# Attention, soft experts and a squared-ReLU layer on one core: another opening of the last stage, and sums moved to GpSimd

## The chip, the core and the metric

The kernel runs on one core of a Trainium2 chip. The metric is the device time of one execution in microseconds, the median of several runs; lower is better. TensorE multiplies matrices into PSUM, VectorE (DVE), ScalarE (ACT) and GpSimd (POOL) work elementwise, and SyncE (SP) issues the transfers. Each engine takes its instructions in the order in which they were put on its queue; semaphores tie the queues together.

## What is computed

Attention over 8 batches of 8 heads (576 positions of 64), causal in blocks of 64; then a soft mixture of 8 experts with 4 slots each over the 4608 tokens of width 512 (c is a softmax over the 32 slots); then a layer 512 to 2048 to 512 with a squared relu.

```python
def _attn_ref(q, k, v):
    ...
def _moe_ref(x, phi, w1, w2):
    ...
    for e in range(E):
        h = np.maximum(slot_input[e] @ w1[e], 0.0)
        slot_out[e] = h @ w2[e]
    ...
    return (c @ slot_out).astype(np.float32)
def _moe2_ref(x, w_in, w_out):
    h = np.maximum(x @ w_in, 0.0)
    return (h * h @ w_out).astype(np.float32)
def reference(**kwargs):
    ...
    attn_out = _attn_ref(**attn_kwargs)
    B, H, S, D = attn_out.shape
    x = np.ascontiguousarray(attn_out.transpose(0, 2, 1, 3)).reshape(B * S, H * D)
    x = _moe_ref(x=x, **moe_kwargs)
    return _moe2_ref(x=x, **moe2_kwargs)
```

## The kernel before

Three stages follow one another: attention (to about 430 us of the trace), the experts (to 464 us) and the last layer. Since the experts' output is a mixture of 32 slot outputs, the last layer's first product is done on the slots: `fold` (L1211) multiplies the slots' outputs with w_in into `psw`, a 128 x 512 tile in PSUM, from the copies `so` of the transposed sums (`finish`, L1203 and L1204). What is left per token is a product with the mixing weights.

**The last stage** (`ffn`). Of the 36 tiles of 128 tokens the first four (N0 = 4, 512 tokens) go through plain f32: `psw` is split into two rounded halves `wf0` and `wf1` (L1402, L1403, L1408, L1409), `spread` (L1418, L1421) brings them into the layout `ws`; for each chunk c = 0 to 7 of the hidden width `first_hidden` (L1441) makes 2 x 128 hidden rows, `relu_square` (L1430, L1431) makes g of them on ScalarE, and `first_product(c, a)` adds four products with the decoded w_out `t` into the four accumulators `pos` (`po`, L1626). Meanwhile w_out arrives and is decoded chunk by chunk (`decode_wo`, `decode_mag`: one ScalarE and four VectorE operations, L234 to L242, and a sum of magnitudes on ScalarE, jk, L1397).

The other 32 tiles form 16 blocks of 256 tokens, whose product with w_out is done in f16 high and low parts by a scheme of seven products in place of eight. It needs seven weight matrices of 128 x 2048: three are quarters of w_out itself, four are sums of quarters. `sum_w` makes the sums, one two-input subtraction of 2048 columns each: T3 writes the tile ta, T4 writes tb, T5 overwrites ta and T6 overwrites tb. `cast_w` (B, L1547, ScalarE) makes the high part bh of each with the scale beta, `low_w` (L, L1550, VectorE) the low part bl. For each block there are four quarters kq of the hidden width: `block_first` (H, L1568, tile ps_hb), `block_square` (q, ScalarE), `block_sums` (s: four sums of 256 columns), `block_cast` (c: ah, two ScalarE casts, the first of four parts, the second of three), `block_low` (l: al, two VectorE subtractions), and then the seven products (P, L1604) and their outputs (E; one sum per block on GpSimd, L1697). The tile pool of ps_h and ps_hb holds two tiles, so that a TensorE step for a third waits until ScalarE has read the first.

**What sets the order.** Under `manual_schedule` the string `ORDER` gives the order on TensorE, VectorE and ScalarE for the end of the first tiles and for the first block: a letter is a step, the digits its arguments (T3 is sum_w(3), q02 is block_square(0, 2), m40 is first_product(4, 0), h7 and g7 are first_hidden and first_square of chunk 7). GpSimd's order is left to the scheduler. The opening of the stage (from psw to chunk c=3) is written out in the code ahead of it, the first tile's work at the pace of ScalarE and VectorE copies:

```python
sub = lambda o, a, b: nc.vector.tensor_tensor(out=o, in0=a, in1=b, op=ALU.subtract)
...
x = tw[s] = tw["p"].tile([128, KH, HM], F32, tag=nm, name=nm) if s < 5 else tw[s - 2]
sub(x, a, b)
```

Of the kernel before, what the change touches and what calls it, by code (L numbers as in the profile page):

```python
# [23 lines left out]
def tile_attn_soft_moe_ffn(  # L24
# [12 lines left out]
    nc = tc.nc  # L37
# [23 lines left out]
    )  # L61
    NTILE = NT // 128
# [166 lines left out]
    def decode_mag(pool, dst, raw, w):  # L229
        hi, lo = raw[:, :, 1], raw[:, :, 0]  # L230
        m = pool.tile([128, w], F32, tag="dec_mag", name="dec_mag")
        b = m.bitcast(U32)
        with tc.high_priority():
            nc.scalar.activation(out=m, in_=hi.bitcast(F32), func=AF.Abs)  # L234
        nc.vector.tensor_scalar(out=m, in0=m, scalar1=2.0 ** -15, scalar2=None, op0=ALU.max)
        nc.vector.tensor_scalar(
            out=b, in0=b, scalar1=3, scalar2=0x3FFFFFF8, op0=ALU.logical_shift_left, op1=ALU.bitwise_and
        )
        nc.vector.scalar_tensor_tensor(
            out=b, in0=hi, scalar=0xC0000000, in1=b, op0=ALU.bitwise_and, op1=ALU.bitwise_or  # L240
        )
# [909 lines left out]
    def experts():  # L1151
# [144 lines left out]
    wos = {}  # L1296
# [67 lines left out]
    def ffn():  # L1364
# [19 lines left out]
        sc = {nm: ws_p.tile([128, 1], F32, name=nm) for nm in ("beta", "alpha", "inv", "sg", "se")}  # L1384
        sc.update(zip(("top", "sw"), cts["tiny"][2:]))
        al = [sc["alpha"]] + cts["tiny"][:2]
        wf = [d_p.tile([128, 512], F32R, name=f"wf{i}", bufs=1) for i in range(2)]
        tt = t_p.tile([128, KH, 2, DM], F32, name="t")

        def decode_wo(c, a=None):  # L1390
            sl = slice(0, 2) if a is None else slice(a, a + 1)
            w = DM * (sl.stop - sl.start)
            raw = wos[c][:, sl].rearrange("p a f x -> p (a f) x")
            decode_mag(d_p, tt[:, c, sl].rearrange("p a f -> p (a f)"), raw, w)
            if a != 0:
                jk = d_p.tile([128, 2, DM], mybir.dt.bfloat16, tag="jk", name="jk", bufs=1)
                nc.scalar.activation(out=jk, in_=tt[:, c], func=AF.Abs, accum_out=sums[:, c:c + 1])  # L1397

        psw = wots["psw"]
        parts = (slice(0, 128), slice(128, 512))  # L1400
        p = parts[0]
        nc.scalar.copy(wf[0][:, p], psw[:, p])  # L1402
        nc.vector.tensor_tensor(out=wf[1][:, p], in0=psw[:, p], in1=wf[0][:, p], op=ALU.subtract)  # L1403
        p = parts[1]
        wfs = cts["w"][:, p]
        nc.scalar.copy(wfs, psw[:, p])
        nc.scalar.copy(cts["w"][:, parts[0]], psw[:, parts[0]])
        nc.gpsimd.tensor_copy(wf[0][:, p], wfs)  # L1408
        nc.gpsimd.tensor_tensor(out=wf[1][:, p], in0=wfs, in1=wf[0][:, p], op=ALU.subtract)  # L1409
        decode_wo(0, 0)  # L1410
# [4 lines left out]
        def spread(c, p=slice(0, 512)):  # L1415
            ps = bank2("ps_ws")
            for i in range(2):
                nc.tensor.matmul(  # L1418
                    ps[:, p], cts["sel"][:, c, 32 * i:32 * i + 128], wf[i][:, p], start=(i == 0), stop=(i == 1)
                )  # L1420
            nc.scalar.copy(ws[:, 512 * c + p.start:512 * c + p.stop], ps[:, p])  # L1421
# [11 lines left out]
        def first_hidden(c, step=1024, late=False):  # L1433
            ps = bank2("ps_h")
            if late:
                hid[c] = lambda: first_square(c, ps)
            else:
                g = g_p.tile([128, 1024], F32, tag="g", name="g")
            for a in range(2):
                f = c + KH * a  # L1440
                nc.tensor.matmul(  # L1441
                    ps[:, 512 * a:512 * a + T0], ws[:, 128 * f:128 * f + 128], ctt[:, 0:T0], start=True, stop=True
                )
                if step == 512:
                    relu_square(ps, g[:, 512 * a:512 * a + 512], 512 * a, 512 * a + 512, scale=1.0 / CSC)
                    if a == 0:
                        spread(2, parts[0])
            if late:
                return
            if step == 1024:  # L1450
                relu_square(ps, g, 0, 1024, scale=1.0 / CSC)
            return g
# [83 lines left out]
        sub = lambda o, a, b: nc.vector.tensor_tensor(out=o, in0=a, in1=b, op=ALU.subtract)  # L1536
# [62 lines left out]
        def product(n, sa, sb, acc, first):  # L1599
# [10 lines left out]
        spread(0, parts[0])  # L1610
        hid = {0: first_hidden(0, 512)}
        decode_wo(0, 1)
        spread(0, parts[1])
        spread(2, parts[1])
        nc.vector.tensor_reduce(
            out=mg[:, 0:1], in_=wf[0].bitcast(F32), axis=AX.X, op=ALU.max, apply_absolute_value=True
        )
        spread(1)
        spread(3)
        for c in range(1, KH):  # L1620
            decode_wo(c)

        def first_product(c, a):
            g = hid[c]
            for t in range(N0):
# [166 lines left out]
```

## Time and profile before

| what | value |
|---|---|
| median of three runs | 865.24 us (864.58 to 865.53) |
| the profiled execution | 864.24 us, of which the span of the trace is 862.4 us |
| granted clock, mean | 0.991 of full speed |
| TensorE busy | 810.9 us, 94% of the span |
| VectorE, ScalarE busy | 670.2 us (78%), 626.9 us (73%) |
| GpSimd busy | 241.5 us (28%), nearly all in the attention stage |
| last stage | 464.2 us to the end |

A busy share says little by itself: the stages have different limits. A timeline row gives the start, the duration, the engine and line, the tiles, and in brackets the idle time before it with what ended it; rows that follow one another without a gap are merged and counted (x16). The chain lists, in order of time, what the last instruction of the kernel waited for, step by step. The granted clock of TensorE has two levels, 1.2 and 2.4 GHz; a slice in which it changed shows a value between 0.50 and 1.00.

### The profile page before, as it was taken

Reading aid. Unit: us, or ns where it says so; the run is one execution under the profiler, and the core shown is the slowest. Engines: PE = TensorE matmul, PEld = TensorE weight load, DVE = VectorE, ACT = ScalarE, POOL = GpSimd, SP = SyncE. Lnnn points to the kernel's source line nnn. Section 1 sums busy time; section 2 is a strip of 40 time slices with the busy share of each in tenths; the row PEclk is TensorE's granted clock in tenths of the full one; section 3 lists DMA queues with packets and bytes.
Section 4 is the critical chain, followed back from the end, with each engine's and each line's share of the span. In section 5 each row is a group of like instructions: output and inputs, shape, how many; then the busy total and the mean of one; then the engine's idle time right before and its main releaser. Section 6 shows DMA issues by size and latency. Waiting matters only on the chain.

```text
span 862.4 us, 21655 instructions
## 1 busy us (share of the span) xinstructions
PE 810.9 (94%) x8741; PEld 597.5 (69%) x8741; DVE 670.2 (78%) x1546; ACT 626.9 (73%) x996; POOL 241.5 (28%) x394
## 2 busy tenths in 40 slices
PE   2699999998999999999986999999999999999997
PEld 1366767575766667676432454888888888888886
DVE  5877789899899987764726899888888888888880
ACT  5588787787878687743225899988888888878770
POOL 0255747376574757464000000000000000000000
PEclk9899999999999999999998999999999999999999
DMA  7997998989898979589899100110000000000002
GB/s 156 194 192 132 186 216 151 223 160 224 156 215 163 197 124 197 90 251 373 335 401 397 57 0 25 39 37 25 26 25 27 25 26 25 26 25 26 26 25 49
DMA packets 213316, 113.14 MB, mean 131 GB/s; under 512 B 192096, under 2 KB 194144, under 8 KB 213216
## 3 DMA queue, kind: packets, MB, share of 16 engines
q1 hardware_dynamic: 210560, 111.11, 54.0%
q8 instruction: 68, 1.11, 0.5%
q10 hardware_dynamic: 2656, 0.66, 0.4%
q14 instruction: 32, 0.26, 0.1%
HBM read 78.71 MB, written 9.44 MB: 102 GB/s over the span
## 4 chain that ended last, share of the span: by engine, by line
PE 73%; DMA 8%; ACT 6%; POOL 6%; DVE 5%; issue 2%; SPq 0%; ACTq 0%; POOLq 0%
PE ps_y L1604 15%; PE ps_z L1604 10%; PE ps_x L1604 10%; PE xm L655 8%; PE ps_sc L581 6%; DMA t<-qb 4%; PE ps_hb L1568 3%; DMA wch<-in_moe_w_dram 3%; PE sm L675 3%; POOL ul L771 3%; PE ps_max L503 2%; POOL ss L624 2%; PE po L1626 2%; PE tl L666 2%; PE ps_qT L482 2%
## 5 line engine op out<-in xcount | busy, mean ns | idle before, releaser
L1604 PEld LDWEIGHTS <-ah 128*128 128x128 f16 x1792 | 174.8, 98 | 21.9 <-issue 0.8
L619 ACT ACTIVATE p<-ps_sc,es 128x512 f32<-128x512 f32 x192 | 129.7, 685 | 59.1 <-PE ps_sc L581 29.8
L1536 DVE TENSOR_TENSOR al<-a,ah 128x1024 f16<-128x1024 f32 (+1 forms) x128 | 138.5, 1124 | 16.9 <-ACT ah L1591 15.3
L517 DVE TENSOR_REDUCE pm<-ps_max 128x4 f32<-128x512 f32 x160 | 106.0, 681 | 32.6 <-PE ps_max L511 32.3
L624 POOL TENSOR_TENSOR ss<-p 128x384 f32<-128x384 f32 (+1 forms) x128 | 85.7, 688 | 152.4 <-ACT p L619 152.0
L1591 ACT CAST ah<-a 128x1024 f16<-128x1024 f32 (+1 forms) x128 | 114.4, 936 | 15.0 <-DVE a L1536 13.4
L581 PE MATMUL ps_sc<-t,s 128*128 128x512 f16 (+3 forms) x512 | 107.0, 302 | 11.7 <-DMA t<-qb 6.6
L1697 POOL TENSOR_TENSOR ot<-u,p 128x256 f32<-128x256 f32 x16 | 12.5, 781 | 373.6 <-DVE u L1668 357.9
L1604 PE MATMUL ps_y<-bh,al 128*128 128x256 f16 x384 | 104.7, 273 | 0.0
L1604 PE MATMUL ps_y<-bh,ah 128*128 128x256 f16 x384 | 104.6, 272 | 0.0
L1604 PE MATMUL ps_y<-bl,ah 128*128 128x256 f16 x384 | 104.6, 272 | 0.0
L624 POOL TENSOR_TENSOR ss<-ss,p 128x320 f32<-128x320 f32 (+1 forms) x128 | 97.9, 765 | 16.9 <-ACT p L619 9.1
L1604 PEld LDWEIGHTS <-al 128*128 128x128 f16 x896 | 87.6, 98 | 10.2
L1430 ACT ACTIVATE r<-ps_hb,cts_h 128x1024 f32<-128x1024 f32 x64 | 71.2, 1112 | 30.0 <-PE ps_hb L1568 29.4
L655 PE MATMUL xm<-p,ar_hi 128*64 128x256 f32 (+3 forms) x512 | 87.2, 440 | 0.0
L1536 DVE TENSOR_TENSOR a<-a 128x256 f32<-128x256 f32 x192 | 76.1, 424 | 3.9
L1604 PE MATMUL ps_x<-bh,ah 128*128 128x256 f16 x256 | 69.8, 273 | 0.0
L1604 PE MATMUL ps_z<-bh,ah 128*128 128x256 f16 x256 | 69.8, 273 | 0.0
L1604 PE MATMUL ps_x<-bh,al 128*128 128x256 f16 x256 | 69.8, 273 | 0.0
L1604 PE MATMUL ps_x<-bl,ah 128*128 128x256 f16 x256 | 69.8, 273 | 0.0
L1604 PE MATMUL ps_z<-bl,ah 128*128 128x256 f16 x256 | 69.8, 273 | 0.0
L1604 PE MATMUL ps_z<-bh,al 128*128 128x256 f16 x256 | 69.8, 273 | 0.0
(275 smaller groups left out, 1779.3 us busy)
## 6 DMA issues: line engine op xcount, KB each, us to landing
wch<-in_moe_w_dram SPq DMA_DIRECT2D x18, 1024.0 KB, 10.9
ar_hi<-in_v_dram SPq DMA_DIRECT2D x64, 128.0 KB, 3.8
raw<-in_moe_w_in_dram SPq DMA_DIRECT2D x16, 512.0 KB, 5.5
out_dram<-ot SPq DMA_DIRECT2D x32, 256.0 KB, 2.1
ar_hi<-in_moe_w_dram SPq DMA_DIRECT2D x6, 1024.0 KB, 7.8
s<-s SPq DMA_DIRECT2D x32, 144.0 KB, 4.1
ar_hi<-in_k_dram SPq DMA_DIRECT2D x16, 256.0 KB, 4.5
ar_hi<-in_q_dram SPq DMA_DIRECT2D x16, 256.0 KB, 4.2
```

The lines of the kernel that those rows point to most:

```text
L517: nc.vector.tensor_reduce(out=o, in_=i, axis=AX.X, op=ALU.max)
L581: nc.tensor.matmul(ps[:, c0:c0 + w].rearrange("p (s c) -> p s c", c=128), kk[:, 2 * t + hp, :], qq[:, 2 * u0 + hp:8:2, :], start=(c0 == 0 ...
L619: exps[:] = [nc.scalar.activation(out=pt, in_=ps, func=AF.Exp, scale=es[:, 0:1])]
L624: add = lambda o, x, y: nc.gpsimd.tensor_tensor(out=o, in0=x, in1=y, op=ALU.add)
L655: nc.tensor.matmul(box["xm"][64 * hp:64 * hp + 64, 128 * t:512], vs[:, t, hp, :], r, start=(t == 0), stop=(t == 3),)
L675: nc.tensor.matmul(SM[b][32 * g:32 * g + 32, o0:o0 + w], oj, r, start=bool(start and j == 0), stop=stop, tile_position=(0, 32 * g), skip_g ...
L771: add = lambda o, x, y: nc.gpsimd.tensor_tensor(out=o, in0=x, in1=y, op=ALU.add)
L1430: nc.scalar.activation(out=r[:, c0:c1], in_=ps[:, c0:c1], func=AF.Relu, **kw)
L1536: sub = lambda o, a, b: nc.vector.tensor_tensor(out=o, in0=a, in1=b, op=ALU.subtract)
L1568: nc.tensor.matmul(ps[:, 512 * j + 256 * a:512 * j + 256 * a + 256], w[:, 128 * f:128 * f + 128], c, start=True, stop=True,)
L1591: nc.scalar.copy(v(hl[n % 2][0][:, 2 * kq:2 * kq + 2], s), v(a7[n, kq], s))
L1604: nc.tensor.matmul(acc[:, 0:HM], a[:, k], b[:, k], start=bool(first and k + j == 0), stop=(k == KH - 1 and j == 2), skip_group_check=not f ...
```

## The change

It has four parts. (1) At the end of the experts the two pairs of transpositions and the folds are ordered anew: the first pair stands before the last four products of the last expert. (2) The opening of the last stage is written out as a function `opening` under manual schedule on three engines: the 384-column split that GpSimd did goes to ScalarE and VectorE, the spreads of two chunks share a tile, the pool ps_o of the accumulators is opened ahead of ps_h (so pos[0] takes the bank that psw had), two groups of fillers (`spin`: 7 and 5 products of constants into pos[0], which the first real product overwrites) stand between the steps, and the first relu and square are halved between ScalarE and VectorE. (3) T4, T5 and T6 run on GpSimd, and so do the sixteen sums of the first block. (4) ORDER is another: the weights' casts come B2 B0 B1, then B3, B4 between the first block's quarters, and T5 stands before B4.

```diff
-        "O h4 n m30 b g4 T3 B2 T4 z m31 B0 a B4 L2 h5 B1 H00 m40 L0 g5 L4 q00 H01 m41 L1 q01 s00 h6 "
-        "B3 H02 s01 m50 c00 T6 c01 m51 l00 g6 l01 q02 h7 L3 g7 H03 m60 s02 q03 T5 m61 c02 s03 B6 "
-        "l02 m70 c03 L6 B5 m71 l03 L5 H10 o0 o1 X P1 q10 H11 o2 s10 P6 F E1 q11 H12 E6 c10 P5 s11 "
+        "O h4 n m30 b g4 T3 B2 T4 z m31 B0 a L2 h5 B1 H00 m40 L0 g5 L1 q00 H01 m41 B3 q01 s00 h6 "
+        "L3 T5 B4 H02 s01 m50 c00 c01 m51 l00 g6 l01 L4 T6 q02 h7 g7 H03 m60 s02 q03 m61 B5 c02 s03 "
+        "L5 l02 m70 c03 B6 m71 l03 L6 H10 o0 o1 X P1 q10 H11 o2 s10 P6 F E1 q11 H12 E6 c10 P5 s11 "
...
+                if c == 7 and kt == 7:
+                    tail.pop(0)()
...
-            pend.append(lambda dts=dts, os_=os_: [finish(1, dts, os_)] + [fold(dt) for dt in dts])
-        pend.pop()()
+            tail.append(lambda dts=dts, os_=os_: finish(1, dts, os_))
+        for f in (lambda: fold(0), tail.pop(0), lambda: fold(1), lambda: fold(2), lambda: fold(3)):
+            f()
...
+        SPINS = (7, 5)
...
-        nc.gpsimd.tensor_copy(wf[0][:, p], wfs)
-        nc.gpsimd.tensor_tensor(out=wf[1][:, p], in0=wfs, in1=wf[0][:, p], op=ALU.subtract)
...
+        ps_o = st.enter_context(tc.tile_pool(name="ps_o", bufs=4, space=PSUM))
         ps_h = st.enter_context(tc.tile_pool(name="ps_h", bufs=2, space=PSUM))
-        ps_o = st.enter_context(tc.tile_pool(name="ps_o", bufs=4, space=PSUM))
...
-            sub(x, a, b)
+            sub(x, a, b, nc.vector if s == 3 else nc.gpsimd)
...
+            e = nc.vector if n else nc.gpsimd
+            e.tensor_tensor(out=z(4), in0=z(1), in1=z(3), op=ALU.add)
+            sub(z(1), z(0), z(1), e)
+            sub(z(5), z(4), z(0), e)
+            sub(z(6), z(2), z(5), e)
...
+        def opening():
+            p0, p1 = slice(0, 128), slice(128, 512)
+            w = cts["w"]
+            nc.scalar.copy(wf[0][:, p0], psw[:, p0])
+            dec.tensor_tensor(out=wf[1][:, p0], in0=psw[:, p0], in1=wf[0][:, p0], op=ALU.subtract)
+            nc.scalar.copy(w, psw)
+            spin(pos[0], SPINS[0])
+            spread((0, 2), p0)
+            nc.scalar.copy(wf[0][:, p1], w[:, p1])
...
+            spin(pos[0], SPINS[1])
+            ps = bank2("ps_h")
...
+            nc.scalar.activation(out=r[:, h0], in_=ps[:, h0], func=AF.Relu, scale=1.0 / CSC)
+            dec.tensor_scalar(
+                out=r[:, h1], in0=ps[:, h1], scalar1=1.0 / CSC, scalar2=0.0, op0=ALU.mult, op1=ALU.max
+            )
```

On GpSimd, whose order the scheduler sets, the end of the attention stage (rows of 64 x 32 and 128 x 240) is followed before by the split of psw and then only by the blocks' outputs (ot):

```order
L943 COPY lg<-ltl 64x32
L1167 MEMSET si 128x240
L1408 CAST wf_8212<-cts_h 128x384
L1409 TENSOR_TENSOR wf_8213<-cts_h,wf_8212 128x384
L1697 TENSOR_TENSOR ot<-u_8823,p_8741 128x256
```

In the change the same place reads so (tb, ta, tb are T4, T5, T6; a_8471, a_8485, a_8530, a_8554 the four quarters of the first block):

```order
L945 COPY lg<-ltl 64x32
L1169 MEMSET si 128x240
L1537 TENSOR_TENSOR tb<-t,ta 128x2048
L1583 TENSOR_TENSOR a_8471<-a_8471 128x2x128
L1537 TENSOR_TENSOR a_8471<-a_8471 128x2x128 x3
L1583 TENSOR_TENSOR a_8485<-a_8485 128x2x128
L1537 TENSOR_TENSOR ta<-t 128x2048
L1537 TENSOR_TENSOR a_8485<-a_8485 128x2x128 x3
L1537 TENSOR_TENSOR tb<-t,tb 128x2048
L1583 TENSOR_TENSOR a_8530<-a_8530 128x2x128
L1537 TENSOR_TENSOR a_8530<-a_8530 128x2x128 x3
L1583 TENSOR_TENSOR a_8554<-a_8554 128x2x128
```

T5 (ta) stands between the first and the last three sums of the second quarter.

On ScalarE before, from the first weight casts to the third quarter's square (a_8516):

```order
L1547 ACTIVATE bh<-t,beta 128x2048 x2
L1547 ACTIVATE bh<-tb,beta 128x2048
L1547 ACTIVATE bh<-t,beta 128x2048
L1430 ACTIVATE r<-ps_h 128x1024
...
L1431 ACTIVATE a_8474<-r 128x2x512
L1547 ACTIVATE bh<-ta,beta 128x2048
L1591 CAST ah_8392<-a_8460 128x2x512
L1591 CAST ah_8392<-a_8460 128x2x384
L1591 CAST ah_8392<-a_8474 128x2x512
L1591 CAST ah_8392<-a_8474 128x2x384
L1430 ACTIVATE r<-ps_h 128x1024
L1431 ACTIVATE g<-r 128x1024
L1430 ACTIVATE r<-ps_hb,cts_h 128x1024
```

and in the change, from the cast of ta on:

```order
L1548 ACTIVATE bh<-ta,beta 128x2048
L1440 ACTIVATE r<-ps_hb,cts_h 128x1024
L1441 ACTIVATE a_8485<-r 128x2x512
L1548 ACTIVATE bh<-tb,beta 128x2048
L1593 CAST ah_8404<-a_8471 128x2x512
L1593 CAST ah_8404<-a_8471 128x2x384
L1593 CAST ah_8404<-a_8485 128x2x512
L1593 CAST ah_8404<-a_8485 128x2x384
L1440 ACTIVATE r<-ps_h 128x1024
L1441 ACTIVATE g<-r 128x1024
L1440 ACTIVATE r<-ps_hb,cts_h 128x1024
L1441 ACTIVATE a_8530<-r 128x2x512
```

The cast of ta moved ahead of the second quarter's relu, that of tb behind its square; the casts of ah keep their place before the relu of chunk c=6 (r<-ps_h) and of the third quarter (r<-ps_hb), and now read what GpSimd writes.

On TensorE before, from the last expert's products on:

```order
L1279 MATMUL po_7991<-wch,hT_7771 4x256 x8
L1203 MATMUL ps_soT<-ident,os 128x128 x2
L1211 MATMUL psw<-tin,so 32x512 x8
L1203 MATMUL ps_soT<-ident,os 128x128 x2
L1211 MATMUL psw<-tin,so 32x512 x8
L1418 MATMUL ps_ws<-wf_8212,sel 128x128
```

and in the change:

```order
L1284 MATMUL po_7991<-wch,hT_7771 4x256 x4
L1205 MATMUL ps_soT<-ident,os 128x128 x2
L1284 MATMUL po_7991<-wch,hT_7771 4x256 x4
L1213 MATMUL psw<-tin,so 32x512 x4
L1205 MATMUL ps_soT<-ident,os 128x128 x2
L1213 MATMUL psw<-tin,so 32x512 x12
L110 LDWEIGHTS ident
L110 MATMUL po<-ident 128x256
```

One pair of transpositions moved between the last expert's products, a fold ahead of the second pair, and fillers (L110) stand between the folds and the first spread.

## Rows read from the trace of the kernel before

**Rows 1.** Stretches: length, busy us (xcount) of PE, PEld, DVE, ACT, POOL, clock, DMA, GB/s.

```profile
476.60:521.00 44.40, 44.34 (x123) 21.77 (x121) 40.52 (x51) 41.30 (x45) 0.00 (x0) 1.00 0.02 7
...
600.00:700.00 100.00, 100.00 (x917) 89.41 (x915) 82.31 (x140) 81.56 (x95) 3.93 (x5) 1.00 0.07 25
```

**Rows 2.** TensorE's timeline: start us, us, line, tile, xcount [idle before <-releaser].

```profile
461.58 0.44 PE L1203 MATMUL ps_soT<-ident,os 128*128 128x128 f32 x2
462.31 1.92 PE L1211 MATMUL psw<-tin,so 128*32 128x512 f32 x16 [0.29 <-DVE so L1204]
466.20 0.44 PE L1418 MATMUL ps_ws<-wf,sel 128*128 128x128 f32 x2 [1.97 <-ACT cts_h L1407]
...
470.14 2.08 PE L1626 MATMUL po<-t,g 128*128 128x512 f32 x2 [2.06 <-ACT g L1431]
...
482.29 1.88 PE L1626 MATMUL po<-t,g 128*128 128x512 f32 x4
```

**Rows 3.** Slices of 1 us: length, busy us (xcount) of TensorE, granted clock, DMA, GB/s.

```profile
468.00:469.00 1.00, 0.07 (x1) 0.63 1.02 406
...
475.00:476.00 1.00, 1.00 (x4) 0.96 1.08 430
```

**Rows 4.** Chain that ended last, 455 to 545 us: start us, us, what.

```profile
515.08 3.44 ACT ah L1591 x4
...
520.56 1.12 ACT r L1430
521.73 0.74 PE ps_hb L1568 x4
522.47 13.74 PE po L1626 x32
```

**Rows 5.** ScalarE's timeline, opening and weight casts.

```profile
464.30 0.27 ACT L1402 CAST wf<-psw 128x128 fp32r<-128x128 f32 x1 [2.65 <-PE psw L1211]
...
497.12 1.02 ACT L1430 ACTIVATE r<-ps_h 128x1024 f32<-128x1024 f32 x1 [1.26 <-PE ps_h L1441]
...
499.14 3.88 ACT L1547 ACTIVATE bh<-t,beta 128x2048 f16<-128x2048 f32 x2
```

**Rows 6.** VectorE's timeline: attention, weight sums, later blocks.

```profile
127.51 1.49 DVE L205 SCALAR_TENSOR_TENSOR tin<-dec_sq,raw 128x512 f32<-128x512 f32 x1
...
499.07 2.29 DVE L1536 TENSOR_TENSOR tb<-t,ta 128x2048 f32<-128x2048 f32 x1
...
502.82 4.61 DVE L1550 SCALAR_TENSOR_TENSOR bl<-t,beta,bh 128x2048 f16<-128x2048 f32 x2
...
512.32 1.22 DVE L1536 TENSOR_TENSOR a<-a 128x256 f32<-128x256 f32 x3
...
552.94 1.63 DVE L1536 TENSOR_TENSOR a<-a 128x256 f32<-128x256 f32 x3
...
611.73 2.10 DVE L1536 TENSOR_TENSOR al<-a,ah 128x1024 f16<-128x1024 f32 x2 [0.32 <-ACT ah L1591]
...
615.79 2.43 DVE L1536 TENSOR_TENSOR al<-a,ah 128x1024 f16<-128x1024 f32 x2
```

**Rows 7.** Spread of one line's durations: GpSimd's sums, and VectorE's L205.

```profile
L624 POOL TENSOR_TENSOR ss<-p x128: 308/922/1282, 36.7 to 402.2; 128x384 f32<-128x384 f32 x64, 128x64 f32<-128x64 f32 x64
L624 POOL TENSOR_TENSOR ss<-ss,p x128: 584/858/1572, 38.7 to 403.5; 128x320 f32<-128x320 f32 x64, 128x192 f32<-128x192 f32 x64
...
L1697 POOL TENSOR_TENSOR ot<-u,p x16: 724/784/787, 552.7 to 853.5; 128x256 f32<-128x256 f32 x16
...
L205 DVE SCALAR_TENSOR_TENSOR tin<-dec_sq,raw x16: 673/1163/1487, 116.1 to 297.8; 128x512 f32<-128x512 f32 x16
```

**Rows 8.** GpSimd's timeline beside the VectorE rows of group 6.

```profile
127.45 1.73 POOL L624 TENSOR_TENSOR ss<-p 128x384 f32<-128x384 f32 x2
...
552.71 0.79 POOL L1697 TENSOR_TENSOR ot<-u,p 128x256 f32<-128x256 f32 x1 [84.61 <-DVE u L1668]
...
615.48 0.79 POOL L1697 TENSOR_TENSOR ot<-u,p 128x256 f32<-128x256 f32 x1 [19.34 <-DVE u L1668]
```

More of the change, by code (lines that the diff above doesn't have):

```diff
@@ L1270, in experts @@
             nc.vector.memset(x, 0.0)
+        tail = []
         for c in range(8):
@@ L1393, in decode_wo, with size @@
             raw = wos[c][:, sl].rearrange("p a f x -> p (a f) x")
[L1394 to L1397, printed above, removed]
+            return decode_mag(d_p, tt[:, c, sl].rearrange("p a f -> p (a f)"), raw, w)
+        def size(c):
+            jk = d_p.tile([128, 2, DM], mybir.dt.bfloat16, tag="jk", name="jk", bufs=1)
+            nc.scalar.activation(out=jk, in_=tt[:, c], func=AF.Abs, accum_out=sums[:, c:c + 1])
@@ L1399, in ffn @@
         psw = wots["psw"]
[L1400 to L1407, printed above, removed]
-        nc.gpsimd.tensor_copy(wf[0][:, p], wfs)
-        nc.gpsimd.tensor_tensor(out=wf[1][:, p], in0=wfs, in1=wf[0][:, p], op=ALU.subtract)
@@ L1410, in ffn, with spread, part @@
-        decode_wo(0, 0)
+        d0, d1 = decode_wo(0, 0), decode_wo(0, 1)
+        for f in d0:
+            f()
         psw_st.close()
+        ps_o = st.enter_context(tc.tile_pool(name="ps_o", bufs=4, space=PSUM))
         ps_h = st.enter_context(tc.tile_pool(name="ps_h", bufs=2, space=PSUM))
-        ps_o = st.enter_context(tc.tile_pool(name="ps_o", bufs=4, space=PSUM))
[L1415 to L1421, printed above, removed]
+        def spread(cs, p=slice(0, 512), run=True):
+            ps = bank2("ps_ws").rearrange("p (a f) -> p a f", a=2)
+            n = p.stop - p.start
+            o = ws.rearrange("p (c f) -> p c f", c=4)[:, cs[0]:4:2, p]
+            def part(x):
+                for i in range(2):
+                    nc.tensor.matmul(
+                        ps[:, x, 0:n], cts["sel"][:, cs[x], 32 * i:32 * i + 128], wf[i][:, p],
+                        start=(i == 0), stop=(i == 1),
+                    )
+            fs = [lambda: part(0), lambda: part(1), lambda: nc.scalar.copy(o, ps[:, :, 0:n])]
+            if not run:
+                return fs
+            for f in fs:
+                f()
@@ L1431, in relu_square, with first_hidden @@
             nc.scalar.activation(out=o, in_=r[:, c0:c1], func=AF.Square)
-        def first_hidden(c, step=1024, late=False):
+        def first_hidden(c, late=False):
             ps = bank2("ps_h")
@@ L1443, in first_hidden @@
                 )
[L1444 to L1452, printed above, removed]
+            if not late:
+                first_square(c, ps)
         def first_square(c, ps):
@@ L1609, in ffn, with first_product @@
         pos = [ps_o.tile([128, DM], F32, tag="o", name="po") for _ in range(N0)]
[L1610 to L1623, printed above, removed]
+        hid = {}
+        def first_product(c, a, ts=range(N0)):
             g = hid[c]
-            for t in range(N0):
+            for t in ts:
                 nc.tensor.matmul(
@@ L1703, in block_out @@
                 store(N0 + 2 * n + 1, ot(1))
-        for c in range(3):
-            hid[c + 1] = first_hidden(c + 1)
-            for a in range(2):
-                first_product(c, a)
+        E = mybir.EngineType
+        dec = nc.vector
+        def opening():
[7 more added lines that the diff above has]
+            nc.scalar.copy(wf[0][:, p1], w[:, p1])
+            for f in d1[:3]:
+                f()
+            dec.tensor_tensor(out=wf[1][:, p1], in0=w[:, p1], in1=wf[0][:, p1], op=ALU.subtract)
+            spin(pos[0], SPINS[1])
+            ps = bank2("ps_h")
+            for a in range(2):
+                nc.tensor.matmul(
+                    ps[:, 512 * a:512 * a + T0], ws[:, 1024 * a:1024 * a + 128], ctt[:, 0:T0], start=True, stop=True
+                )
+            pre = spread((0, 2), p1, False)
+            pre.pop(0)()
+            r = o_p.tile([128, 1024], F32, tag="r", name="r", bufs=1)
+            g = hid[0] = g_p.tile([128, 1024], F32, tag="g", name="g")
+            h0, h1 = slice(0, 256), slice(256, 512)
+            nc.scalar.activation(out=r[:, h0], in_=ps[:, h0], func=AF.Relu, scale=1.0 / CSC)
+            dec.tensor_scalar(
+                out=r[:, h1], in0=ps[:, h1], scalar1=1.0 / CSC, scalar2=0.0, op0=ALU.mult, op1=ALU.max
+            )
+            nc.scalar.activation(out=g[:, h0], in_=r[:, h0], func=AF.Square)
+            dec.tensor_tensor(out=g[:, h1], in0=r[:, h1], in1=r[:, h1], op=ALU.mult)
+            d1[3]()
+            first_product(0, 0, (0, 1))
+            pre.pop(0)()
+            first_product(0, 0, (2, 3))
+            ds = decode_wo(1)
+            nc.scalar.activation(out=r[:, 512:1024], in_=ps[:, 512:1024], func=AF.Relu, scale=1.0 / CSC)
+            nc.scalar.activation(out=g[:, 512:1024], in_=r[:, 512:1024], func=AF.Square)
+            pre.pop(0)()
+            first_product(0, 1, (0,))
+            first_hidden(1)
+            first_product(0, 1, (1, 2, 3))
+            for f in ds:
+                f()
+            dec.tensor_reduce(
+                out=mg[:, 0:1], in_=wf[0].bitcast(F32), axis=AX.X, op=ALU.max, apply_absolute_value=True
+            )
+            spread((1, 3))
+            size(0)
@@ L1709, in ffn @@
+        with tc.manual_schedule(engines={E.PE, E.DVE, E.Activation}):
+            opening()
+        size(1)
+        for c in range(2, KH):
+            for f in decode_wo(c):
+                f()
+            size(c)
+        with tc.manual_schedule(engines={E.PE}):
+            for c in range(1, 3):
+                first_hidden(c + 1)
+                for a in range(2):
+                    first_product(c, a)
         E = mybir.EngineType
```

30 lines of the change are left out of this document (13 added, 17 removed).

## The prediction

> **What bounds the kernel now.** I read the busy time by stretch first. In 600 to 700 us TensorE is busy 100.00 of 100.00 us [rows 1], and the next hundred reads the same: once the blocks of the last stage run, they end when TensorE has done its work, and whatever delays or advances the first block passes to the end one to one. So the question is when the first block's first product starts: 536.5 now, straight behind 32 records of po [rows 4]. Before that, in 476.6 to 521, ScalarE is busy 41.30 of 44.40 us, VectorE 40.52, GpSimd 0.00 [rows 1]: two full engines and an empty one, and TensorE looks busy (44.34) only because f32 products fill it.
>
> Next TensorE's timeline at the opening. The folding of the experts' sums into psw ends at 462.31 + 1.92 = 464.23; then TensorE waits 1.97 us for a ScalarE copy, and 2.06 us before the first po at 470.14 [rows 2]. Its clock pays for that: the slice 468 to 469 shows 0.63 and 475 to 476 shows 0.96 [rows 3], so it ran at 1.2 in place of 2.4 GHz from about 468.3 to 475.1, of which 4.95 us lie in dense work: some 2.5 us of work lost.
>
> Last the chain of waits before the first block: the ah casts on ScalarE, relu and square of the last first-tile hidden c=6, relu of the block's third quarter (q02), then TensorE at 521.73 and po from 522.47 on [rows 4]. That gate, **q02's relu frees the PSUM tile of H03**, is what I follow through the change.
>
> **The change, part by part.**
>
> *Tail of the experts.* A fold waits for VectorE's copy of the transposed sums, 0.29 us [rows 2]; there are two such waits (the other is 0.28), and a pair of transpositions of 0.44 stands between them [rows 2]. The change does one pair before the last expert's final products and puts a fold in front of the second pair, which takes all three off: 0.28 + 0.29 + 0.44 = 1.0 us; psw is ready at 463.2.
>
> *Opening.* From 463.2: ScalarE's 128-column cast 0.27 [rows 5], VectorE's difference (about the same, at the end of which the copy of 512 columns is under way). By the cast's 0.27 and 3.88 for two of 2048 columns [rows 5] the copy costs some 0.6. The fillers write the bank that psw had, so they wait for that copy: 464.4. Seven fillers at the pace of a 256-column record, 0.11 each, end at 465.2; four spreads at 0.2 (0.44 for two at full clock [rows 2]) 466.0; the ws cast 0.4, in which the five other fillers run, 466.4; two hidden products 467.0; relu and square, halved between ScalarE and VectorE, 0.4 each: first po near 467.9, against 470.14. With the clock kept, the eight po of c=0 (0.86 each: 13.74 for 32 records of 0.43 [rows 4], two records each), six spread pairs and the hidden products of two chunks are 6.9 + 1.2 + 0.9 = 9.0: c=1 starts at 476.9, against 482.29 [rows 2]. The opening thus gains 5.4 us, the 1.0 above included. Were the clock lost here too, it would be 2.9.
>
> *What is late next.* ScalarE has 3.1 us free in 476.6 to 521 [rows 1] and VectorE's decoding of w_out is not shortened; the weight casts need beta, which stands behind the last decoded chunk and comes near 497 as before: ta's sum of 2.29, next on VectorE, ended at 499.07 there [rows 6]. Before, relu and square of chunk 4 stood there first, the relu from 497.12 after 1.26 us of waiting for TensorE [rows 5]; with TensorE ahead they are done by then, and the first cast starts at 497.2 against 499.14 [rows 5]. Of 5.4 us, 1.95 arrive there and the rest turns into short TensorE waits. From here on the gain at most is 2 us.
>
> *Sums given to GpSimd.* VectorE is rid of three sums of 2.29 [rows 6] and sixteen of 0.41 (1.22 for three [rows 6], merged): 13.5 us in all. What they cost on GpSimd: without VectorE beside it, its two-input sums took 308 ns at 64 columns and 584 at 192 (the least of each form) and 724 at 256 [rows 7]; that is 2.16 ns a column on 170 ns, and 4.59 us for 2048 columns, an estimate that extends the line eightfold. (The Trainium skill, GPSIMD Engine Reference, section 3.1, gives 4497 ns on GpSimd and 2293 on VectorE for this width; no row shows the first, VectorE's 2.29 agrees; by it each large sum would be 0.1 us shorter, and that page's section 4.1 advises VectorE for such work.) *Beside VectorE* both lose. Three small sums took 1.63 in place of 1.22 where a GpSimd sum overlapped the first of them (552.94 to 553.50): 0.41 lost in 0.56. Two al took 2.43 in place of 2.10, overlapped for 0.48 us: 0.33 lost [rows 6, 8]. VectorE lost about 0.7 of the overlap, while GpSimd took 784 for 724 ns [rows 7]. In the attention stage the split is another: 1.49 for an operation whose least is 0.67 [rows 6, 7], so 0.55 of the overlap, and GpSimd 1.73 [rows 8] for a pair that the line above puts at 1.00 + 0.31. So per us of overlap VectorE loses 0.47 to 0.72 and GpSimd stretches by 1.1 to 1.35. A 4.6 us sum then takes over 3 us from VectorE, to spare it 2.3.
>
> *The walk.* GpSimd: T4 (needs ta, from VectorE at 499.4) ends between 504.4 and 505.6; four sums of the first quarter from 507.2, 0.8 to 1.1 each, and the first of the second quarter at 511.2 to 511.6. VectorE: scales to 500.8, then three bl of 2.3 (4.61 for two [rows 6]), overlapped by 4 to 5.5 us of T4 and by those sums; each us costs 0.5 to 0.7: they end at 512.4 to 513.2 in place of 507.7. The bl of ta (2.34) ends near 515. **T5 overwrites ta, so GpSimd waits for that bl**, and behind T5 stand the last three sums of the second quarter. T5 runs beside al: 5.2 to 5.9, ends 520.7. One sum: 521.5. The cast of that quarter (c01) on ScalarE has waited since 514.7; its second half needs two sums more and ends at 523.9. Behind it on ScalarE are relu and square of c=6 (to 526.0) and q02's relu (1.1, [rows 4]): 527.1. Then H03 and po at 527.6, against 522.3: **+5.3 us**. The two splits of the contention give the same within 0.1, since what one engine loses the other wins. TensorE has then stood since 517.4 (its po of c=0 to 6 end there) with 0.43 us of work in over 10 us. In the opening of before it fell to half speed about 4 us after its dense work ended, though it had more to do in between; so I expect the same here from 521.5 on, and the same price, 2.45 us. In 497 to 521 before there was no such gap. After H03 everything is TensorE's: 32 po records, first product. The sums of the last two quarters and al end at 542.6, behind po at full clock (541.8) by up to 0.8, before it at half clock (544.2).
>
> Sum against the profiled execution: 864.24 + 5.3 + 2.45 = 872.0. The median of the runs, 865.24, stands 1.0 above it, and the prediction is for a median: **873.0**. Bounds: with T5 and the sums a quarter less stretched, 3.6 and no clock loss, 868.8; with a quarter more and the clock loss, 876.
>
> **Rivals.** (1) *Contended, clock kept*: 865.24 + 5.3 = 870.5, or 871 with the late al. For it: the granted clock shows one fall in this stage only; against: the gap here is longer than that one and emptier. (2) *GpSimd and VectorE do not disturb each other in these forms.* Then the three bl end at 507.7, bl of ta follows its cast (511.4), T5 runs 511.9 to 516.5, c01 is done at 519.4, H03 at 522.7: +0.9, so 866.1, and 868.6 if the clock falls all the same. Against it: two kinds of this very stage's subtractions slowed [rows 6]. (3) *Faster*: GpSimd does 2048 columns at VectorE's 2.29 and small sums at 0.41. T5 then ends by 513.8, c01 waits for nothing, the 1.95 us that the casts lead stay, and with ScalarE's small gaps H03 comes 2.3 us earlier: 862.9. It decides at a T5 end of about 515.3: in the walk H03 comes 6.4 us behind T5's end, and before it came at 521.73 [rows 4]; the least times of GpSimd [rows 7] say no. (4) *The opening does not do what it says*: the fillers wait for the psw copy, delay the spreads and the clock falls nonetheless. It costs 2.5 us at c=1, but 3.4 of the opening's 5.4 are lost to ScalarE in any case, so the end moves by under 0.5; it changes no sign.
>
> **How the numbers follow.** Contended with the clock lost, 0.50 (870 to 876); contended with the clock kept, 0.21 (868.8 to 871.5); undisturbed, 0.14, half within 0.2% and half above; faster, 0.09; a longer delay by something unseen (a second gap before the sixth product, which needs the last bl), 0.06, above 876. A difference of 0.2% (1.7 us) is about what a measurement can tell from none. Faster 0.09, same 0.08, slower 0.83. The range, 866.0 to 876.0, leaves out the faster case, the longer delay and a little of the undisturbed one.
>
> **What would show it.** In the changed kernel: po of c=1 near 477 and no slice under 1.00 in 464 to 476 (opening right); the first bh cast near 497; GpSimd's T4 of 5 to 6 us and its bl's neighbours of 3 to 5 us in place of 2.34 (contention); ScalarE waiting for GpSimd at the second ah pair for 5 to 7 us; TensorE idle for about 7 us before the hidden product of c=7, and slices of 0.5 in 522 to 532. I am wrong if T5 ends before 517, or if ScalarE meets no GpSimd wait at c01. A time under 864 would mean that the opening's gain passed through ScalarE, which I hold full.

## The result, and the profile after

The changed kernel takes 875.75 us (873.07 to 879.67, six runs) against 864.91 us of the kernel before in the same comparison: 1.0133 times as long, 95% interval 1.0111 to 1.0154. It is slower, as forecast; the delay is 11 us and not the forecast 7.8, so that the ratio applied to 865.24 gives 876.7, just above the range's end of 876.0. The profiled execution took 875.69 us, 11.45 more than that of before, on a span of 873.9.

The start of the last stage differs by some us from execution to execution (the wait for the last expert's weights ended between 456.0 and 462.5 us in the profiles shown here), so distances are counted from the end of psw where it matters. TensorE's timeline of the changed kernel, to be set beside [rows 2] and [rows 4]:

```profile
464.36 0.92 PE L110 MATMUL po<-ident 128*128 128x256 f16 x7 [1.33 <-ACT cts_h L1704]
...
467.88 1.98 PE L1617 MATMUL po<-t,g 128*128 128x512 f32 x4 [0.21 <-ACT g L1726]
...
477.05 7.03 PE L1617 MATMUL po<-t,g 128*128 128x512 f32 x16
...
527.29 1.22 PE L1449 MATMUL ps_h<-cts,ws 128*128 128x512 f32 x2 [9.30 <-ACT r L1440]
529.53 1.22 PE L1569 MATMUL ps_hb<-cts,ws 128*128 128x256 f32 x4 [1.01 <-ACT r L1440]
530.55 15.05 PE L1617 MATMUL po<-t,g 128*128 128x512 f32 x32
...
548.08 0.27 PE L1606 MATMUL ps_x<-bh,ah 128*128 128x256 f16 x1 [2.01 <-ACT ot L1624]
```

The opening does what the prediction said of it: fillers behind the copy of psw, first po at 467.88 (forecast 467.9), c=1 at 477.05 (476.9). Then TensorE stands for 9.30 us ahead of the last hidden product of the first tiles, and once more for 2.01 us ahead of the first block's product, which starts at 548.08 in place of 536.52. By stretches (length, busy us of TensorE, weight loads, VectorE, ScalarE, GpSimd, clock, DMA, GB/s):

```profile
464.00:476.60 12.60, 11.93 (x45) 6.80 (x45) 10.70 (x17) 8.71 (x13) 0.00 (x0) 1.00 1.03 409
476.60:521.00 44.40, 39.47 (x107) 18.58 (x105) 41.19 (x41) 36.97 (x40) 17.86 (x7) 1.00 0.02 6
521.00:550.00 29.00, 19.68 (x60) 10.29 (x61) 17.32 (x10) 20.03 (x20) 19.04 (x13) 0.82 0.04 13
600.00:700.00 100.00, 100.00 (x917) 89.39 (x916) 81.70 (x141) 81.53 (x95) 3.92 (x5) 1.00 0.08 28
```

No low clock in the opening, where before had some; between 521 and 550 the clock is 0.82 and TensorE idles for over 9 us. From 600 on all is as in [rows 1], so the delay of the first product is the delay of the kernel: 548.08 - 536.52 = 11.56 against 11.45. What TensorE waited for is on ScalarE:

```profile
497.31 5.79 ACT L1548 ACTIVATE bh<-t,beta 128x2048 f16<-128x2048 f32 x3 [0.98 <-DVE beta L1477]
...
517.47 0.83 ACT L1593 CAST ah<-a 128x768 f16<-128x768 f32 x1 [3.22 <-POOL a L1537]
524.00 1.04 ACT L1593 CAST ah<-a 128x1024 f16<-128x1024 f32 x1 [5.70 <-POOL a L1537]
...
544.83 0.83 ACT L1593 CAST ah<-a 128x768 f16<-128x768 f32 x1 [2.02 <-POOL a L1537]
545.56 2.00 ACT L1548 ACTIVATE bh<-tb,beta 128x2048 f16<-128x2048 f32 x1
547.47 1.05 ACT L1624 COPY ot<-po 128x512 f32<-128x512 f32 x2
```

The weights' casts start at 497.31 (forecast 497.2), then the casts ah of the first block wait for GpSimd's sums, 3.22 and 5.70 us at a time, and in the second half 3.25 and 2.02 us. GpSimd and VectorE beside each other, 499 to 545:

```profile
499.61 4.55 POOL L1537 TENSOR_TENSOR tb<-t,ta 128x2048 f32<-128x2048 f32 x1 [83.10 <-DVE ta L1537]
507.52 2.78 POOL L1583 TENSOR_TENSOR a<-a 128x256 f32<-128x256 f32 x1 [3.36 <-ACT a L1441]
510.38 7.05 POOL L1537 TENSOR_TENSOR a<-a 128x256 f32<-128x256 f32 x3
...
518.09 4.49 POOL L1537 TENSOR_TENSOR ta<-t 128x2048 f32<-128x2048 f32 x1
522.54 2.92 POOL L1537 TENSOR_TENSOR a<-a 128x256 f32<-128x256 f32 x3
...
537.28 2.77 POOL L1583 TENSOR_TENSOR a<-a 128x256 f32<-128x256 f32 x1
540.14 4.66 POOL L1537 TENSOR_TENSOR a<-a 128x256 f32<-128x256 f32 x3
```

```profile
499.40 0.42 DVE L1483 TENSOR_REDUCE m<-ps_mg 128x2 f32<-128x256 f32 x1
499.85 4.33 DVE L1486 SCALAR_TENSOR_TENSOR se<-m 128x1 f32<-128x1 f32 x1
...
505.11 7.34 DVE L1551 SCALAR_TENSOR_TENSOR bl<-t,beta,bh 128x2048 f16<-128x2048 f32 x3
512.37 2.82 DVE L1551 SCALAR_TENSOR_TENSOR bl<-ta,beta,bh 128x2048 f16<-128x2048 f32 x1
...
518.33 5.05 DVE L1537 TENSOR_TENSOR al<-a,ah 128x768 f16<-128x768 f32 x1 [1.48 <-ACT ah L1593]
```

Two rows tell the mechanism. An operation of **one column** on VectorE (line 1486, 0.16 us elsewhere) took 4.33 us: it began 0.24 us after T4 and ended with it. And T4 itself took 4.55 us, just what the line through GpSimd's undisturbed rows gave (4.59), though VectorE stood ready beside it all the while. Later it is GpSimd that waits: a sum of 256 columns, 0.72 us alone, took 2.78 beside bl of 2.34. Nobody is slowed; they take turns, instruction by instruction. T5 too took 4.49, and the al beside it, 0.95 us alone for 768 columns, took 5.05. The Trainium skill (SBUF — State Buffer, Who interferes with whom) says so: VectorE instructions with two SBUF inputs contend with GpSimd's that read SBUF for a shared pair of ports, "an exclusive lock", and whoever comes first keeps it for the whole instruction. These rows agree (4.33 us for one column, T4 at its undisturbed 4.55); the prediction had overlooked that section.

### The profile page after: what moved, and what is told of

Same layout as the page of the kernel before. It is cut to its first block, busy times and chain, and to the rows that moved or that the text cites. A ratio compares the mean times of both kernels' runs of the same rounds, so it can differ in the third digit from the quotient of the medians.

```text
span 873.9 us, 21679 instructions
## 1 busy us (share of the span) xinstructions
PE 812.3 (93%) x8753; PEld 598.3 (68%) x8753; DVE 670.2 (77%) x1530; ACT 626.7 (72%) x993; POOL 275.6 (32%) x411
## 4 chain that ended last, share of the span: by engine, by line
PE 74%; POOL 9%; DMA 6%; DVE 5%; ACT 4%; issue 2%; SPq 1%; ACTq 0%; POOLq 0%
PE ps_y L1606 14%; PE ps_x L1606 10%; PE ps_z L1606 10%; PE xm L657 7%; PE ps_sc L583 6%; DMA t<-qb 4%; PE ps_hb L1569 3%; PE sm L677 3%; POOL ul L773 3%; PE ps_max L505 2%; PE ps_u L764 2%; POOL ss L626 2%; PE tl L668 2%; POOL a L1537 2%; PE ps_qT L484 2%
## 5 line engine op out<-in xcount | busy, mean ns | idle before, releaser
L1537 DVE TENSOR_TENSOR al<-a,ah 128x1024 f16<-128x1024 f32 (+1 forms) x128 | 144.9, 1172 | 21.8 <-ACT ah L1593 20.2
L1537 DVE TENSOR_TENSOR a<-a 128x256 f32<-128x256 f32 x180 | 71.5, 424 | 3.6
```

The costliest lines, as they stand in the source:

```text
L1537: sub = lambda o, a, b, e=nc.vector: e.tensor_tensor(out=o, in0=a, in1=b, op=ALU.subtract)
```

## The experiments

Three theories: **A (turns)**, as just told; **B (shares)**, the prediction's, by which both engines run on slowed; **C**, that the opening and the new order cost the time and not GpSimd. Numbers of first products under A were walked along the queues with that rule.

**One half of the move each, and none of it.** In the first, T4 to T6 return to VectorE:

```diff
-            sub(x, a, b, nc.vector if s == 3 else nc.gpsimd)
+            sub(x, a, b, nc.vector)
```

> The changed kernel with T4, T5 and T6 back on VectorE; the sixteen sums of the first block stay on GpSimd. Theory A (turns: a GpSimd sum and a two-input VectorE instruction never run side by side, each waits for the end of the other's whole instruction, as 4.33 us for a one-column operation beside T4 suggest): every small sum waits for a whole bl or al, so the first block's first product starts near 539.4 with full clock (548.1 in the changed kernel, 536.5 before), some 3 us slower than before: 868, and up to 870.5 if the clock falls in the 5 us gap. Theory B (shares: both run on, slowed in part, as the prediction had it): the small sums cost 0.3 to 0.5 us each and the first product starts near 534.5: 863. Theory C (the opening and the new order are what costs, not GpSimd): the time stays near 875.

Measured: 869.55 us, ratio 1.0050 (1.0029 to 1.0071). That lies between A's two figures (868 and 870.5); B and C are some 6 us off on either side. The four small sums of one quarter now take GpSimd 9.27 us (506.56 to 515.83), about what VectorE needs for four bl (of 2.34 each):

```profile
506.56 1.05 POOL L1583 TENSOR_TENSOR a<-a 128x256 f32<-128x256 f32 x1 [91.17 <-ACT a L1441]
507.69 8.14 POOL L1537 TENSOR_TENSOR a<-a 128x256 f32<-128x256 f32 x3
```

In the second the small sums return:

```diff
-            e = nc.vector if n else nc.gpsimd
+            e = nc.vector
```

> The changed kernel with the sixteen sums of the first block back on VectorE; T4, T5, T6 stay on GpSimd. Theory A (turns): VectorE stands for 4.3 us at T4 and again at T5, first product near 540.3 at full clock: 868.9, up to 871.5 if the clock falls in the gap of 6 us. Theory B (shares): near 536.5: 865. Theory C (opening and order): near 875.

Measured: 872.93 us, ratio 1.0092 (1.0066 to 1.0119): A's direction, 1.4 us above its upper figure. The sums of the second quarter, on VectorE now, meet T5 (three of them, 1.22 us alone), and ScalarE waits for them:

```profile
517.68 5.40 DVE L1537 TENSOR_TENSOR a<-a 128x256 f32<-128x256 f32 x3
```

```profile
522.37 1.78 ACT L1593 CAST ah<-a 128x1024 f16<-128x1024 f32 x2 [5.90 <-DVE a L1537]
```

In the third both edits are made:

> The changed kernel with nothing on GpSimd: the opening, the tail and the new order alone. Theories A and B, which agree here: ScalarE and VectorE carry what they carried before, the casts of ta and tb stand ahead of the first tile's relu, and the 2 us by which they start earlier are used up: first product near 536.6, time 865.0 within 0.7. No slice of low clock in the opening. Theory C (opening and order cost the 11 us): near 875.

Measured: 866.58 us, ratio 1.0021 (1.0005 to 1.0037), 1.6 above the figure. So about 9 of the 11 us go with GpSimd; theory C falls. The 1.6 us are taken up below, under the clock.

**The move alone**, in the kernel before with its own opening and order (the two edits above, turned round):

> The kernel before with the move to GpSimd alone: T4, T5, T6 and the sixteen sums of the first block, with its own opening and order. Theory A (turns): VectorE stands for 4.3 us at T4 and again beside T6, the small sums wait for one bl or al each, first product near 548 in place of 536.5: 874 to 877. Theory B (shares): near 542.6: 871. Theory C (the move only hurts together with the new order): under 867.

Measured: 877.47 us, ratio 1.0156 (1.0124 to 1.0187), 0.5 above theory A's upper figure and 6.5 above B's. The first product came 83.61 us after psw (545.47 - 461.86), 11.3 later than before, where A's line had 11.5. The one-column operation (line 1485 there) took 2.23 us this time: it began 2.30 us into T4 (4.53 us) and ended with it. T6, which began 0.17 us behind a bl of 2.35 us, took 6.57. So the move costs as much without the rest of the change, 12.7 us.

**Turns or shares, by themselves.** The three large sums on GpSimd in eight pieces:

```diff
-            sub(x, a, b, nc.vector if s == 3 else nc.gpsimd)
+            for k in range(1 if s == 3 else KH):
+                k = slice(None) if s == 3 else k
+                sub(x[:, k], a[:, k], b[:, k], nc.vector if s == 3 else nc.gpsimd)
```

> The changed kernel with T4, T5 and T6 on GpSimd in eight pieces of 256 columns each. Theory A (turns, one instruction at a time): VectorE's one-column operation beside T4 (line 1486 of the changed kernel, 4.33 us there) waits for one piece only, at most 0.8 us; beside bl of 2.3 us each piece waits for a whole bl, so T4, which had 4.55 us to itself, ends several us later; the first product, which then waits for more turns, starts about 1.5 us later than in the changed kernel. Theory B (shares of one path, by bytes): the one-column operation stays as long as before or is not slowed at all, and T4 takes 8 x 0.72 = 5.8 us and no more than 1.3 times that.

Measured: 875.93 us in one run. VectorE's rows, then GpSimd's:

```profile
499.19 0.51 DVE L1486 SCALAR_TENSOR_TENSOR se<-m 128x1 f32<-128x1 f32 x1
499.62 0.14 DVE L1489 TENSOR_SCALAR cts_h<-m 128x1 f32<-128x1 f32 x1
...
500.57 0.52 DVE L1497 SCALAR_TENSOR_TENSOR inv<-se 128x1 f32<-128x1 f32 x1
501.01 8.37 DVE L1553 SCALAR_TENSOR_TENSOR bl<-t,beta,bh 128x2048 f16<-128x2048 f32 x3
```

```profile
498.96 13.74 POOL L1537 TENSOR_TENSOR tb<-t,ta 128x256 f32<-128x256 f32 x8 [83.12 <-DVE ta L1537]
```

The one-column operation waits for a piece (0.51) and no longer for the whole; T4 now loses its turn to three bl and takes 13.74 us, and each bl some 0.5. That is theory A; B had at most 7.5 us. The later start of the first product that A's line expected came in part: 85.89 us after psw (548.30 - 462.41) against 85.04 in the unsplit kernel (548.08 - 463.04), 0.9 us of the 1.5. The time cannot tell one run from the unsplit kernel. And the operations of lines 1489 to 1492, with one input from SBUF, kept their 0.14 to 0.15 us beside the running pieces, while line 1497, with two, took 0.52. Line 1493, with two as well, took 0.16: it began at 500.30, just before one piece ended and the next began (two pieces fill 499.64 to 501.07). So of these small operations it is the two-input ones that wait.

**Does a GpSimd instruction with one input take its turn too?**

```diff
-            sub(x, a, b, nc.vector if s == 3 else nc.gpsimd)
+            if s == 3:
+                sub(x, a, b)
+            else:
+                nc.gpsimd.tensor_copy(out=x, in_=a)
```

> The changed kernel with T4, T5 and T6 on GpSimd replaced by plain copies of their first operand (so the output leaves the second operand of three weight sums out): same tiles, same waits, one input in place of two. Theory A1 (any GpSimd instruction on SBUF keeps VectorE's two-input instructions out): the one-column operation of line 1486 still waits until the copy's end, 2 to 4 us. Theory A2 (only two-input GpSimd instructions do): it takes 0.16 us, as before, and c01 on ScalarE waits less for GpSimd.

Measured: 868.15 us in one run. The copy of T4 no longer needs ta, so it ran earlier and met another one-column operation, that of beta:

```profile
495.34 1.89 POOL L1545 COPY tb<-t 128x2048 f32<-128x2048 f32 x1 [80.04 <-ACT jk L1405]
```

```profile
496.07 1.17 DVE L1477 SCALAR_TENSOR_TENSOR beta<-sg 128x1 f32<-128x1 f32 x1
...
499.81 0.16 DVE L1486 SCALAR_TENSOR_TENSOR se<-m 128x1 f32<-128x1 f32 x1
```

1.17 us, to the end of the copy at 497.23: theory A1, on another row than foreseen; line 1486 itself, with GpSimd idle, took 0.16.

**The clock after the gap.** The kernel with nothing on GpSimd has two short waits on TensorE, 1.87 and 1.50 us, and then the clock falls for some 3.4 us (its rows, then its slices with busy us, clock, DMA, GB/s):

```profile
520.12 0.73 PE L1449 MATMUL ps_h<-cts,ws 128*128 128x512 f32 x2 [1.87 <-ACT r L1440]
522.36 0.76 PE L1569 MATMUL ps_hb<-cts,ws 128*128 128x256 f32 x4 [1.50 <-ACT r L1440]
```

```profile
522.00:523.00 1.00, 0.65 (x5) 0.97 0.00 0
523.00:524.00 1.00, 1.00 (x3) 0.50 0.00 0
...
526.00:527.00 1.00, 1.00 (x3) 0.82 0.00 0
527.00:528.00 1.00, 1.00 (x3) 1.00 0.00 0
```

```diff
+        def fill(k):
+            for _ in range(k):
+                nc.tensor.matmul(pos[0][:, 0:256], zero, warm, start=False, stop=False, skip_group_check=True)
...
-                "h": lambda c: first_hidden(c, late=True),
+                "h": lambda c: (fill(17) if c == 7 else None, first_hidden(c, late=True)),
...
-                "H": block_first,
+                "H": lambda n, kq: (fill(14) if (n, kq) == (0, 3) else None, block_first(n, kq)),
```

> The kernel with nothing on GpSimd (866.6) with 31 more fillers on TensorE, products with zeros added into an accumulator, in the two waits ahead of the hidden products of c=7 and of the block's last quarter. If the fall of the granted clock after that gap is what it lost against the opening alone, all slices from 516 to 530 show 1.00, the 32 po records after H03 take 13.9 us in place of 15.6, and the time is 864.9. If the gap and not the clock cost, 866.6 stays.

Measured: 864.86 us, ratio 1.0001 (0.9979 to 1.0022), the figure expected. TensorE's rows of the two kernels, without and with the fillers:

```profile
522.93 15.59 PE L1617 MATMUL po<-t,g 128*128 128x512 f32 x32
```

```profile
516.80 2.02 PE L1399 MATMUL po<-ident,zero 128*128 128x256 f16 x17
...
521.66 13.89 PE L1624 MATMUL po<-t,g 128*128 128x512 f32 x32
```

15.59 to 13.89, with every slice from 516 to 530 at 1.00, and the first product 73.89 us after psw (535.86 - 461.97) in place of 75.61 (538.84 - 463.23): the 1.7 us between the expected 865 and the measured 866.6 of the kernel without GpSimd were the clock, for which that expectation had allowed nothing. The two times alone would not show it, since their intervals overlap. What the new order loses beyond that against the opening alone (1.4 us from psw to the first product, by the next run's 72.45) was not looked into.

**The opening alone**, with the order of before:

> The opening and the tail alone: nothing on GpSimd and the order of before behind the opening. The products of c=1 start at 477.0 as in the changed kernel (482.3 before). If ScalarE is the bound from 477 to 521, 1.6 us of the 5.3 arrive: first product near 535.0 and 863.3. If the gain passes whole, 859.9; if all of it is lost at ScalarE, 865.

Measured: 863.82 us, ratio 0.9983 (0.9968 to 0.9997). From psw's end the first product comes after 72.45 us (538.52 - 466.07), before after 72.29 (536.52 - 464.23): what arrives is the gain of the tail (1.2 us by the traces: psw ends 4.55 us after the wait for the last weights, before 5.77), and of the opening's own gain nothing.

**The fillers left out of it** (SPINS = (0, 0)):

> The opening alone, as in the run of that name, without the twelve fillers. Theory F (the fillers keep the clock): without them a slice of the granted clock under 1.00 shows within 5 us of the first po, the products of c=1 start up to 2.5 us later; the time moves by under 0.6 us (864.0 against 863.8), since ScalarE holds the stage from there on. Theory G (the opening is short enough without them): no slice under 1.00, c=1 within 0.3 us, the same time.

Measured: 862.89 us, ratio 0.9979 (0.9957 to 1.0001), and once more:

> The opening alone without fillers once more, beside the new order on one chip: 862.9, 1.8 us or 0.2% below the kernel before.

Measured: 862.16 us, ratio 0.9974 (0.9958 to 0.9990). No slice under 1.00 in the opening: theory G as to the clock. But c=1 started 12.62 us after psw (479.68 - 467.06) in place of 14.01 (480.08 - 466.07), 1.4 us earlier, where G had it within 0.3 and F later; neither theory had foreseen that the fillers themselves cost time. They wait for the copy of psw, which the spread does not need, and hold the spread back:

```profile
463.29 2.78 PE L1213 MATMUL psw<-tin,so 128*32 128x512 f32 x24
467.40 0.93 PE L110 MATMUL po<-ident 128*128 128x256 f16 x7 [1.33 <-ACT cts_h L1704]
468.08 0.64 PE L1422 MATMUL ps_ws<-wf,sel 128*128 128x128 f32 x4
```

```profile
464.28 2.78 PE L1213 MATMUL psw<-tin,so 128*32 128x512 f32 x24
467.45 0.87 PE L1422 MATMUL ps_ws<-wf,sel 128*128 128x128 f32 x4 [0.39 <-ACT wf L1702]
```

The first po comes 3.45 us after psw in place of 4.84 (470.51 - 467.06, 470.91 - 466.07), and 1.1 of that stays up to the weights' first cast and the first product (71.3 us after psw). VectorE's decoding takes part in it. With the fillers VectorE stands for a cast that is itself late:

```profile
469.65 0.56 DVE L1710 TENSOR_TENSOR wf<-cts_h,wf 128x384 fp32r<-128x384 f32 x1 [1.40 <-ACT wf L1707]
```

Without them this wait is gone, and the last decoding operation ends 30.95 us after psw in place of 32.09. So what holds the stretch from 468 to 495 is not ScalarE alone.

**A version from these runs**: that opening without fillers, nothing on GpSimd, and an order in which the scale's small operations go ahead of T4 and casts that only the first product needs go behind the relu that frees a PSUM tile:

```diff
-        "O h4 n m30 b g4 T3 B2 T4 z m31 B0 a B4 L2 h5 B1 H00 m40 L0 g5 L4 q00 H01 m41 L1 q01 s00 h6 "
-        "B3 H02 s01 m50 c00 T6 c01 m51 l00 g6 l01 q02 h7 L3 g7 H03 m60 s02 q03 T5 m61 c02 s03 B6 "
+        "O h4 n m30 b T3 z g4 B0 a H00 m40 B2 T4 h5 B1 m31 L0 L2 q00 H01 g5 B4 m41 L1 q01 h6 s00 B3 "
+        "L4 m50 s01 c00 m51 H02 l00 L3 g6 H03 q02 T6 c01 h7 g7 l01 m60 s02 q03 m61 c02 s03 m70 T5 l02 "
...
```

> The opening without fillers, nothing on GpSimd, and another order: the scale's small VectorE operations ahead of T4, the ScalarE casts that only the first product needs (c00, c01, the bh of ta and tb) behind the relu and square that free TensorE's PSUM tiles. TensorE's waits between 484 and the first product, 0.4, 1.3, 1.1, 0.7 and 1.6 us in the opening without fillers, should shrink to 0.4, 1.3 and 1.0: 2.3 us less, 860.6 against 862.9. If the casts moved back then hold up the first product, the gain goes there and the time stays at 862.9.

Measured: 860.16 us, ratio 0.9952 (0.9928 to 0.9976): faster than both kernels, by 4.6 us and 15.6 us in the medians, and close to the 860.6 expected. Of the waits only these are left between 484 and the first product, which comes 68.75 us after psw (533.07 - 464.32) against 71.28 in the opening without fillers (533.84 - 462.56); which of the moves in the order brought how much was not separated:

```profile
484.83 7.13 PE L1617 MATMUL po<-t,g 128*128 128x512 f32 x16 [0.16 <-ACT g L1441]
...
497.05 0.49 PE L1471 MATMUL ps_mg<-ident,mg 128*128 128x128 f32 x2 [1.20 <-DVE mg L1466]
...
518.30 0.73 PE L1449 MATMUL ps_h<-cts,ws 128*128 128x512 f32 x2 [0.79 <-ACT r L1440]
```

## Why the prediction was wrong in size

By its own steps:

- *Tail and opening*: right, to 0.2 us at the first po and c=1, and the clock held. That most of the gain would be lost by the weights' casts was right too (497.31 against 497.2). The prediction named ScalarE as full and VectorE's decoding as not shortened; the run without fillers showed that the decoding takes part. That run also shows rival 4 half true: the fillers delay the spreads, and the first product by 1.1 us where the rival had the end move by under 0.5, but the clock did not fall with or without them.
- *GpSimd's price alone*: right (4.55 against 4.59; 0.72 for 256 columns).
- *Beside VectorE*: here it failed. "So per us of overlap VectorE loses 0.47 to 0.72 and GpSimd stretches by 1.1 to 1.35" reads a mean off rows in which one instruction had simply waited for another: the 0.79 us sum in [rows 8] began 0.31 us ahead of the al of [rows 6], which lost 0.33 of the 0.48 us that were left of it. (No row gives the 0.47; the rows read there give 0.55 to 0.73.) The loss of the one and the stretch of the other depend on who comes first and on the other's length, and a short sum beside bl waits for a whole bl. So the signs named for sharing did not show: T4 took 4.55 us and not 5 to 6, the bl beside the sums 2.45 on the mean of three and 2.82, not 3 to 5. In their place the small sums, for which the walk had 0.8 to 1.1 us, took 2.3 to 2.8. That put T5's start at 518.1 in place of 515 and its end at 522.6 in place of 520.7, though T5 itself took 4.49 and not 5.2 to 5.9. The gate, H03, came at 529.5 in place of 527.1: +7.8 and not +5.3 against [rows 4].
- *"After H03 everything is TensorE's"*: failed for the same reason. The last quarter's four sums on GpSimd took 2.77 and 4.66 us beside bl and al, so its casts ended at 545.7, the bh of tb (2.00) and a copy of po followed on ScalarE, and the first product stood 2.01 us for them. From H03 to the first product it took 18.55 us in place of 14.79.
- *The clock*: fell as forecast, at 522.6, and came back at 532.9 (by the slices 522 to 523, 0.81, and 532 to 533, 0.57). Of the forecast 2.45 us it cost 1.6 behind H03: H03 itself 0.4 (po started 1.02 us after it in place of 0.58) and the 32 po records 1.2 (15.05 in place of 13.9 at full clock, as in the kernel with the fillers). With ScalarE's chain behind it these 1.6 would probably have been hidden in any case; no run shows that. In the kernel without GpSimd the fall showed its price, 1.7.
- *Sum*: 7.8 to H03, 1.6 of clock, 2.0 of waiting and 0.2 at the handover to the first product, 11.6 in place of 5.3 + 2.45. A clock term 0.9 too large hid a part of what the contention and the last wait were short of. The rival "GpSimd and VectorE do not disturb each other" is out, and so is the faster one: GpSimd did not come near 2.29 for 2048 columns.

Not tried: the large sums on GpSimd at a place where VectorE has nothing with two inputs to do.

## What to carry to other kernels

Work on SBUF given to an idle GpSimd is not hidden behind a VectorE that is busy with two-input work on SBUF (here even a GpSimd copy, with one input, took its turn): count the two engines' work as one queue, and add for every short instruction up to one whole long one of the other engine. An instruction's delay beside another that shares something with it should be read from its start and end against the other's, not as a rate. And a gain ahead of a full engine is worth only what that engine can use: here, in medians, 1.1 us of the 5 with the fillers and 1.8 to 2.6 without them, until the order behind it was changed as well.

## What the runs showed of the hardware

- A one-column VectorE operation with two inputs took 4.33 us beside a GpSimd sum of 2048 columns, 0.51 beside pieces of 256, 1.17 beside a GpSimd copy; one-input operations beside the pieces and beside the copy kept 0.14 to 0.15.
- GpSimd's copy of 128 x 2048 f32 took 1.89 us, its two-input sum of that size 4.49 to 4.57, and 6.57 where it began 0.17 us behind a VectorE bl of 2.35.
- In the kernel with nothing on GpSimd, waits of 1.87 and 1.50 us with 0.73 of work between were followed by a fall to 1.2 GHz, which came at 522.9, when dense work had begun again, and lasted 3.4 us. With products with zeros, added into an open accumulator in those waits, every slice stayed at 2.4 GHz.
